# Batch 0's pooling in a written order, weights in halves and a new work list in an attention-and-maxout kernel

## The chip, the cores and the metric

The kernel runs on one core of one Trainium2 chip. The metric is the device time of one execution in microseconds (us); the median over several runs counts. Where a profile is read, times run from the start of its span. TensorE does the matrix products, VectorE and ScalarE the elementwise work, GpSimd and SyncE issue transfers (GpSimd adds some sums of its own).

## The reference, cut to what matters

```python
# x: (4, 12544, 128), inducing: (32, 128), w1, w2: (128, 1024), w_out: (1024, 128)
def mab(q, kv):
    s = scale * (q @ kv.transpose(0, 2, 1))       # scale = 1/sqrt(128)
    a = softmax(s)                                # over the rows of kv
    return a @ kv
h   = mab(inducing, x)     # pooling: 32 rows for each batch
y   = mab(x, h)            # each token attends to its batch's 32 rows
h1  = y @ w1
h2  = y @ w2
out = maximum(h1, h2) @ w_out                     # (50176, 128) float32
```

The kernel uses max(h1, h2) = h1 + relu(h2 - h1). The attention of a token over 32 rows is folded into the weights: for each batch, hwd = h (w2 - w1) is a 32 x 1024 matrix, and m1 = h w1 w_out a 32 x 128 one. What is left for a token are its 32 exponentials e, relu(e hwd) w_out + e m1, and a division by the sum of e at the end.

## The kernel before, in words

**Tiles.** A batch has 98 tiles of 128 tokens. Two buffers xT hold a batch's x turned (channels on the partitions), twelve tiles xn hold x as it comes, in 16 bits, each with 14 tiles of 128 tokens.

**Loading.** x comes by GpSimd's queue, which also makes 16 bits of it (`load_x`, L182). Batch 0 comes in eleven parts, `parts[0]` (L175): four of 14 tiles, four of 7, then 6, 5 and 3; the very first comes by SyncE and is cast by VectorE and ScalarE. Behind batch 0 the same queue loads w1, w2 and w_out (L240 to L242), then batch 1's seven parts (L765) and w1 and w2 once more in 32 bits (L548, L549), from which GpSimd makes w2 - w1 for the later batches.

**Batch 0's pooling** (L724 to L764) is the head of the kernel. For each part, `p1_transpose` turns it on TensorE (two halves, evicted by VectorE, L266, and ScalarE, L269), `p1_scores` multiplies with the 32 inducing rows and takes the exponential on ScalarE (L278, L287), and `p1_accum` sums up (L301 for the denominators, L310 for the rows of h). The parts go through these steps in a fixed pattern, with filling matmuls that compute nothing needed (`fill`, L720) between some of them. Then come the small steps: w1 is negated on VectorE (L768), `small_h` makes hT4 (h turned and repeated four times, L455), `weights_2` turns w1 in two groups of four blocks into w1T (L562), `small_sums` makes the reciprocals rs and rw (L481 to L486), `stage` makes the first e, and `small_hwd` the first half of hwd (L501 to L516).

**Batches 1 to 3** are pooled while the main work of the batch before runs. Their x is turned by transposing transfers of SyncE: `transpose_x_dma` (L200), eleven for each batch, x1.0 to x1.10 for batch 1, the first eight of 7 tiles, the last three of 14. `pool_scores` (c, L338) takes 16 tiles of xT at a time: c1.0 takes tiles 0 to 15, and x1.0, x1.1 and x1.2 bring tiles 0 to 6, 7 to 13 and 14 to 20. `pool_turn` (t) turns the exponentials with another transfer, `pool_accum` (a, L396) sums.

**Main work.** Up to 16 tiles form a block of four quarters. `stage` (s, L625) makes a block's e: TensorE multiplies in four column strips, ScalarE takes the exponential. `phase` (p, L1009) multiplies e with pieces of hwd in up to four row strips of TensorE at the same time; each unit fills a PSUM bank (128x512), and ScalarE (L1024) or VectorE (L1027) evicts it with a relu. p4 is a phase with four units, the figure behind the dot says which of its evictions change the engine. In phases with fewer than four units a strip may do the "linear" product e m1 for one group. `final_one` (L859) multiplies 128 columns of relu with a block of w_out: 3,136 of them, eight for each tile. When a group of up to four tiles is done, `evict_group` multiplies with the reciprocal of the sum on VectorE (L891) into one of five output tiles (`NOUT`), and SyncE stores it (L918). The sums of e come from another transposing transfer on SyncE (`turn_e2`, g, L651) and additions on GpSimd, or, for the first blocks, from TensorE (`dens`, L704).

**What sets the order.** All five engines run in a written order. The main work follows the word list `ORDER`: a number stands for so many final matmuls, a letter for a step (s, p, c, t, a, x, g as above; H the second half of batch 0's hwd; W, w, e, h, m small steps of weights and batches), and each word emits its instructions on every engine it uses, SyncE's queue too. A small model of the engines' times, `Clock`, is kept along the way: it chooses PSUM banks and eviction engines, and it says when filling matmuls are put in. Its estimates have no effect on the chip beyond that. The stores and all transposing transfers of SyncE stand in one queue, in the order of the list.

Of the kernel before, what the change touches and what calls it, by code (L numbers as in the profile page):

```python
# [16 lines left out]
INF = 1e9  # L17
NOUT = 5


class Clock:
# [4 lines left out]
    LAT = 0.20  # L26
    SEM = 0.05

    def __init__(self):
        self.pe = self.act = self.dve = self.sp = 0.0  # L30
        self.pool = self.loading = self.loaded = 0.0
        self.stored = [0.0] * NOUT
        self.mode = "full"
        self.bank = [0.0] * 8
        self.idle = {}
        self.log = []
        self.busy = {}
# [45 lines left out]
class Block:  # L83


    def __init__(self, quarters, full=()):
# [3 lines left out]
        self.staged = None  # L90
        self.divided = 0.0
# [32 lines left out]
def kernel(  # L124
# [50 lines left out]
    parts[0] = [(0, 14), (14, 14), (28, 14), (42, 14), (56, 7), (63, 7), (70, 7), (77, 7), (84, 6), (90, 5), (95, 3)]  # L175
# [41 lines left out]
    w1h = relup.tile([128, 4096], F16, name="w1h", tag="relu1")[:, 0:J]  # L217
    w21 = consts.tile([C, J], F16, name="w21")
    woutp = consts.tile([128, NJB, C], F16, name="woutp")
    w1T = consts.tile([128, NJB, C], F16, name="w1T")  # L220
# [6 lines left out]
    with tc.manual_schedule(engines={ET.PE, ET.DVE, ET.Activation, ET.Pool, ET.SP}):  # L227
# [12 lines left out]
        nc.gpsimd.dma_start(out=w1h, in_=moe_w1)  # L240
        nc.gpsimd.dma_start(out=w2h, in_=moe_w2)
# [11 lines left out]
        def p1_transpose(b, i, between=0):  # L253
            k0, n = parts[b][i]
            xn = xn_at[b, i]
            h = min(8, (n + 2) // 2)
            for g, m in ((0, h), (h, n - h)):
                if g and between:
                    fill(between)
                bi, ps = bank([128, 8, 128], F16)  # L260
                for j in range(m):
                    nc.tensor.transpose(ps[:, j, :], xn[:, g + j, :], identity16)  # L262
                end = ck.run(0.056 * m, ready=ck.bank[bi], why="T")
                dst = xT_tiles[b % 2][:, k0 + g : k0 + g + m, :]
                if g == 0:
                    nc.vector.tensor_copy(out=dst, in_=ps[:, 0:m, :])  # L266
                    ck.bank[bi] = ck.on_dve(end, 0.08 + 0.075 * m)
                else:
                    nc.scalar.copy(out=dst, in_=ps[:, 0:m, :])  # L269
                    ck.bank[bi] = ck.on_act(end, 0.05 + 0.12 * m)  # L270
                st[b]["xT", i] = max(ck.bank[bi], st[b].get(("xT", i), 0.0))

        def p1_scores(b, i):
# [11 lines left out]
            end = ck.run(0.029 * n)  # L285
# [5 lines left out]
        def p1_accum(b, i, lo=0, hi=P1):  # L291
# [4 lines left out]
            if b == 0:  # L296
# [20 lines left out]
                st[0]["end"] = ck.run(0.029 * (hi - lo) + 0.03 * ((hi - lo + 3) // 4))  # L317
# [132 lines left out]
        def small_h(b):  # L450
            hT4 = smp.tile([C, 4, M], F16, name=f"hT4_{b}", tag="hT4")
            if b == 0:
# [9 lines left out]
                st[b]["hT4r"] = ck.on_dve(st[0]["end"], 0.3)  # L462
# [3 lines left out]
                ready = ck.on_act(st[0]["end"], 0.2)  # L466
# [10 lines left out]
        def small_sums(es, ready):  # L477
# [9 lines left out]
            ck.bank[st[0]["eb"]] = st[0]["rsr"] = ck.on_dve(end, 0.34)  # L487

        def small_hwd(b, halves=(0, 1), vector=False):
            if 0 in halves:  # L490
                st[b]["hwd"] = smp.tile([128, J], F16, name=f"hwd_{b}", tag="hwd")
            hwd = st[b]["hwd"]
            for half in halves:
                for n in range(2 if b == 0 and half == 0 else 1):
                    w = 256 if b == 0 and half == 0 else 512
                    bi, ps = bank([128, 512])
                    ps = ps[:, 0:w]
                    sl = slice(512 * half + w * n, 512 * half + w * (n + 1))
                    ck.wait(max(ck.bank[bi], st[b]["hT4r"]), "p1")
                    if b == 0:  # L500
                        nc.tensor.matmul(out=ps, lhsT=st[b]["hT4"], rhs=w2h[:, sl], start=True, stop=False)  # L501
                        nc.tensor.matmul(out=ps, lhsT=st[b]["hT4"], rhs=w1h[:, sl], start=False, stop=True)
                        end = ck.run(0.43 * w / 512)
                    else:
                        nc.tensor.matmul(out=ps, lhsT=st[b]["hT4"], rhs=w21[:, sl], start=True, stop=True)  # L505
                        end = ck.run(0.215)
                    if half == 0 and n == 0 or vector:
                        if b == 0:
                            nc.vector.tensor_scalar(
                                out=hwd[:, sl], in0=ps, scalar1=st[0]["rw"], scalar2=None, op0=ALU.mult  # L510
                            )
                        else:
                            nc.vector.tensor_copy(out=hwd[:, sl], in_=ps)
                        ck.bank[bi] = ck.on_dve(end, 0.07 + w / 970.0)
                    else:
                        nc.scalar.activation(  # L516
                            out=hwd[:, sl], in_=ps, func=AF.Copy, scale=st[0]["rw"] if b == 0 else 1.0
                        )
                        ck.bank[bi] = ck.on_act(end, 0.06 + w / 1200.0)
                    st[b]["hw", half] = max(ck.bank[bi], st[b].get(("hw", half), 0.0))  # L520
# [35 lines left out]
        def weights_2():  # L556
            for g in range(2):
                bi, ps = bank([128, 4, 128], F16)
                ck.wait(ck.bank[bi], "w")
                for j in range(4):  # L560
                    jb = 4 * g + j
                    nc.tensor.transpose(ps[:, j, :], w1h[:, 128 * jb : 128 * (jb + 1)], identity16)  # L562
                end = ck.run(0.056 * 4)
                if g == 0:
                    nc.vector.tensor_copy(out=w1T[:, 0:4, :], in_=ps)
                    ck.bank[bi] = ck.on_dve(end, 0.4)
                else:
                    nc.scalar.copy(out=w1T[:, 4:8, :], in_=ps)
                    ck.bank[bi] = w_of["w1T"] = ck.on_act(end, 0.5)
# [41 lines left out]
        def stage(blk):  # L611
# [29 lines left out]
            blk.staged = ck.bank[bi] = ck.on_act(end, 0.05 + wd * 128 / 1200.0)  # L641

# [89 lines left out]
        for i in range(4):  # L732
            p1_transpose(0, i, 2 if i == 0 else 0)
            if i < 3:
                fill(2 - i // 2)
            if i == 0:
                bi, ps = bank([128, 512])
                nc.tensor.transpose(ps[:, 0:M], ind_sb, identity32[0:M, 0:M])
                nc.vector.tensor_copy(out=inducingT, in_=ps[:, 0:M])
                ck.bank[bi] = 0.0  # L740
                nc.vector.reduce_sum(out=diag, in_=identity32.rearrange("p (k m) -> p m k", m=M), axis=AX.X)
                for dst, f in ((rep32, DOWN / scale), (repd, 1.0)):
                    nc.vector.tensor_scalar(
                        out=dst.rearrange("p (k m) -> p k m", m=M),
                        in0=diag[:, None, :].broadcast_to((128, 4, M)),
                        scalar1=f,
                        scalar2=None,
                        op0=ALU.mult,
                    )
            if i > 0:  # L750
                p1_accum(0, i - 1)
            p1_scores(0, i)
        last = len(parts[0]) - 1
        p1_transpose(0, 4)
        p1_accum(0, 3)
        p1_transpose(0, 5)
        p1_scores(0, 4)
        for i in range(6, last + 1):
            p1_transpose(0, i)
            p1_scores(0, i - 1)  # L760
            p1_accum(0, i - 2)
        p1_scores(0, last)
        p1_accum(0, last - 1)
        p1_accum(0, last)  # L764
# [18 lines left out]
        for n, g in enumerate(groups):  # L783
            g.blk.last_group[g.q] = n
        state.update({"g": 0, "mm": 0, "done": 0, "issued": 0})
# [95 lines left out]
        def evict_group(g, end):  # L881
# [3 lines left out]
            qs = sorted({q for q, _ in g.chunks})  # L885
            per = n // len(qs)
            t0 = g.chunks[0][1]
            rp = g.blk.rp[:, t0 : t0 + per, qs[0] : qs[-1] + 1]
            if len(qs) == 1:
                rp = rp.broadcast_to((128, per, C))  # L890
                nc.vector.tensor_mul(osb[:, 0:n, :], g.ps[:, 0 : n * C].rearrange("p (s c) -> p s c", s=n), rp)  # L891
            elif per == 1:
                rp = g.blk.rp[:, t0, qs[0] : qs[-1] + 1]
                nc.vector.tensor_mul(
                    osb[:, 0:n, :],
# [227 lines left out]
```

## Time and profile before

| | |
|---|---|
| median of 3 runs | 317.46 us (317.13 to 318.28) |
| the profiled execution | 318.49 us, its span 316.7 us |
| TensorE busy | 311.5 us, 98% of the span |
| ScalarE busy | 279.0 us, 88% |
| VectorE busy | 273.6 us, 86% |
| GpSimd busy | 127.5 us, 40% |
| matmuls | 5,309, of them 3,136 finals |
| last sum of batch 0's pooling ends | 22.48 us |
| first final matmul | 26.89 us |
| granted TensorE clock | 1.00 |

In lists of instructions a line gives start, duration, engine, source line, operation, what it writes and reads, and a count. "PEld" is TensorE's load of weights, which lies beside its matmuls; "SPq" is SyncE's queue of transfers: the time there is that of issuing, not of the transfer. A line of busy times by stretch has, for TensorE, its weight loads, VectorE, ScalarE and GpSimd, the busy microseconds (with the number of instructions), then the granted clock, the DMA share and GB/s. A line of the chain gives start, duration and what the end of the program hung on at that time. Lines of DMA queues give packets, MB and share of 16 engines; q0 is GpSimd's queue and q1 is SyncE's.

### The profile page before, as it was taken

The numbers are of one execution on the slowest core, as the hardware profiler recorded it, in microseconds if no ns is written. First come the engines' busy times: TensorE is split into PE (matmuls) and PEld (weight loads), VectorE is DVE, ScalarE is ACT, GpSimd is POOL, SyncE is SP. The second block draws the span as 40 slices with busy tenths as digits, with TensorE's granted clock in tenths as the row PEclk, the third lists the DMA queues.
The fourth block names the chain that finished last, engine by engine and source line by source line (L and its number), as shares of the span: only waits on it lengthen the run. The fifth ranks groups of instructions, "written<-read, shape, count | busy, mean of one in ns | idle before, by whom it ended". The sixth has DMA issues, their size and how long they took to land.

```text
span 316.7 us, 12562 instructions
## 1 busy us (share of the span) xinstructions
PE 311.5 (98%) x5309; PEld 240.8 (76%) x5309; DVE 273.6 (86%) x486; ACT 279.0 (88%) x571; POOL 127.5 (40%) x189
## 2 busy tenths in 40 slices
PE   8999999999999999999999999999999999999996
PEld 3885767777877768778777787887868777787885
DVE  2348989999888899998988998889899989989995
ACT  2669999999999999998999989999899999998881
POOL 7442071648510066067320064449305663461500
PEclk9999999999999999999999999999999999999999
DMA  8999999999699998997399998995423233324223
GB/s 205 209 206 212 226 232 213 225 239 217 120 215 244 234 175 175 198 234 205 113 216 243 179 248 212 229 187 169 139 85 118 85 120 118 119 79 146 104 103 117
DMA packets 81480, 56.34 MB, mean 178 GB/s; under 512 B 62832, under 2 KB 66064, under 8 KB 81424
## 3 DMA queue, kind: packets, MB, share of 16 engines
q1 hardware_dynamic: 75312, 41.32, 56.6%
q0 software_dynamic: 6112, 14.22, 23.1%
q8 instruction: 41, 0.67, 1.0%
q14 instruction: 15, 0.12, 0.1%
HBM read 28.33 MB, written 25.69 MB: 171 GB/s over the span
## 4 chain that ended last, share of the span: by engine, by line
PE 95%; ACT 1%; DMA 1%; DVE 1%; issue 1%; DVEq 0%; ACTq 0%
PE ps L859 61%; PE ps L1009 23%; PE ps L625 2%; PE ps L262 2%; PE ps L338 2%; PE ps L396 1%; DMA xf<-in_x_dram 1%; PE ps L278 1%; PE ps L310 1%; PE ps L720 1%; PE ps L301 1%; PE ps L505 0%; PE ps L441 0%; ACT hwd L516 0%; ACT relu L1024 0%
## 5 line engine op out<-in xcount | busy, mean ns | idle before, releaser
L1024 ACT ACTIVATE relu<-ps 128x512 f16<-128x512 f32 x472 | 242.9, 619 | 20.8 <-PE ps L1009 18.9
L1027 DVE TENSOR_SCALAR relu<-ps 128x512 f16<-128x512 f32 x312 | 198.5, 684 | 19.4 <-PE ps L1009 18.6
L859 PE MATMUL ps<-woutp,relu 128*128 128x128 f16 x3136 | 204.0, 219 | 0.0
L859 PEld LDWEIGHTS <-relu 128*128 128x128 f16 x3136 | 176.6, 98 | 34.2 <-issue 28.7
L1009 PE MATMUL ps<-e,hwd 32*128 32x512 f16 (+2 forms) x880 | 85.3, 357 | 0.0
L660 POOL TENSOR_TENSOR half<-ed 128x256 f32<-128x256 f16 (+2 forms) x23 | 14.1, 613 | 126.9 <-DMA ed<-e 126.6
L664 POOL TENSOR_TENSOR rd<-den,minus 128x16 f32<-128x16 f32 (+2 forms) x23 | 60.7, 2639 | 1.9
L891 DVE TENSOR_TENSOR o<-ps,rd 128x512 f32<-128x512 f32 (+1 forms) x88 | 55.5, 633 | 4.1 <-PE ps L1009 2.4
L1009 PEld LDWEIGHTS <-hwd 32*128 32x128 f16 x880 | 28.0, 91 | 18.4 <-issue 5.1
L1009 PE MATMUL ps<-m,e 32*128 32x128 f16 x382 | 38.5, 216 | 0.0
L1009 PEld LDWEIGHTS <-e 32*128 32x128 f16 x382 | 22.6, 92 | 5.4 <-issue 1.7
L660 POOL TENSOR_TENSOR half<-half 128x32 f32<-128x32 f32 (+3 forms) x69 | 22.3, 323 | 5.4
L187 POOL DMA_DIRECT2D xn<-in_x_dram x31 | 17.0, 557 | 7.3 <-DMA xn<-in_x_dram 4.5
L891 DVE TENSOR_TENSOR o<-ps,rp 128x512 f32<-128x512 f32 (+3 forms) x20 | 12.9, 644 | 1.1 <-DMA out_dram<-o 0.8
L266 DVE COPY xT<-ps 128x512 f16<-128x512 f16 (+3 forms) x11 | 5.5, 504 | 8.3 <-PE ps L262 8.1
L637 ACT ACTIVATE e<-ps 128x512 f16<-128x512 f32 (+2 forms) x21 | 11.0, 596 | 0.2 <-PE ps L625 0.2
L351 ACT ACTIVATE eu<-ps 128x512 f16<-128x512 f32 x18 | 11.1, 615 | 0.1
L269 ACT COPY xT<-ps 128x768 f16<-128x768 f16 (+3 forms) x11 | 6.1, 557 | 3.6 <-PE ps L262 3.4
L625 PE MATMUL ps<-xT,hT 128*32 128x512 f16 (+3 forms) x114 | 8.8, 363 | 0.1
L262 PE MATMUL ps<-identity,xn 128*128 128x128 f16 x98 | 7.8, 226 | 0.1
L262 PEld LDWEIGHTS <-xn 128*128 128x128 f16 x98 | 6.0, 101 | 1.7 <-DVE xn L724 1.0
L338 PE MATMUL ps<-xT,inducingT 128*32 128x512 f16 x72 | 7.1, 386 | 0.0
(100 smaller groups left out, 112.4 us busy)
## 6 DMA issues: line engine op xcount, KB each, us to landing
out_dram<-o SPq DMA_DIRECT2D x90, 256.0 KB, 2.7
xn<-in_x_dram POOLq DMA_DIRECT2D x24, 448.0 KB, 11.8
out_dram<-o SPq DMA_DIRECT2D x10, 128.0 KB, 2.6
xn<-in_moe_w_dram POOLq DMA_DIRECT2D x4, 256.0 KB, 14.0
xn<-in_x_dram POOLq DMA_DIRECT2D x4, 224.0 KB, 9.6
xT<-xn SPq DMA_TRANSPOSE x33, 4.4
xf<-in_x_dram SPq DMA_DIRECT2D x1, 512.0 KB, 3.7
xf<-in_x_dram SPq DMA_DIRECT2D x1, 384.0 KB, 4.2
```

The source lines that it names most:

```text
L187: nc.gpsimd.dma_start(out=xn_at[b, i][:, 0:n, :], in_=xr[b, :, k0 : k0 + n, :])
L262: nc.tensor.transpose(ps[:, j, :], xn[:, g + j, :], identity16)
L338: nc.tensor.matmul(out=ps[32 * g : 32 * (g + 1), :], lhsT=inducingT, rhs=xT_tiles[b % 2][:, U * u + 4 * g : U * u + 4 * (g + 1), :], start ...
L351: nc.scalar.activation(out=eu, in_=ps, func=AF.Exp, scale=scale, accum_out=st[b]["es"][:, u : u + 1])
L625: nc.tensor.matmul(out=ps[32 * q : 32 * (q + 1), 128 * t : 128 * (t + n)], lhsT=hq, rhs=xT[:, c : c + n, :], start=True, stop=True, tile_p ...
L660: nc.gpsimd.tensor_tensor(out=dst, in0=cur[:, :, 0:n], in1=cur[:, :, n : 2 * n], op=ALU.add)
L664: nc.gpsimd.tensor_tensor(out=rp[:, 0:wd, :].rearrange("p t q -> p (t q)"), in0=den[:, 0 : 4 * wd], in1=minus1[:, 0 : 4 * wd], op=ALU.pow,)
L859: nc.tensor.matmul(out=g.ps[:, 128 * c : 128 * (c + 1)], lhsT=g.blk.relu[g.q][:, 128 * (jb * w4 + t) : 128 * (jb * w4 + t + 1)], rhs=woutp ...
L891: nc.vector.tensor_mul(osb[:, 0:n, :], g.ps[:, 0 : n * C].rearrange("p (s c) -> p s c", s=n), rp)
L1009: nc.tensor.matmul(**seq[i])
L1024: nc.scalar.activation(out=dst, in_=src, func=AF.Relu)
L1027: nc.vector.tensor_scalar(out=dst, in0=src, scalar1=0.0, scalar2=None, op0=ALU.max)
```

## The change

1. Batch 0 comes in twelve parts: the last three of 6, 5 and 3 tiles become four of 6, 4, 2 and 2. Its pooling follows a written list, `HEAD` (1a is the first half of part 1's transposes, S1 its scores, A1 its sum, I the inducing rows, N the negation of half of w1). Two of the seven filling matmuls stay.
2. w1 and w2 come in two halves each, and w1 is negated in halves (`negate`). w1T lies in the unused part of w1's buffer, and `weights_2` is split into a half before the list and a half in its first word, H.
3. Batch 0's hwd is made in three pieces of 256, 256 and 512 columns, the first two before the list, all evicted by VectorE. The first block's e is made in two halves of 256 columns (`stage_first`), and a unit waits for the half and the pieces that it reads.
4. `phase` writes the matmuls of its strips in the order in which their banks and inputs come free by the model, instead of in turn.
5. `evict_group` gives six of 107 groups to ScalarE (up to four activations of 128 columns each) by a written string, `EVICT`. There are six output tiles.
6. `ORDER` is a new list. The model's figures are changed too (landing times of batch 0's and batch 1's x, some durations).

The core of the diff:

```diff
-NOUT = 5
+NOUT = 6
...
-    parts[0] = [(0, 14), (14, 14), (28, 14), (42, 14), (56, 7), (63, 7), (70, 7), (77, 7), (84, 6), (90, 5), (95, 3)]
+    parts[0] = [(0, 14), (14, 14), (28, 14), (42, 14), (56, 7), (63, 7), (70, 7), (77, 7), (84, 6), (90, 4), (94, 2), (96, 2)]
...
-            st[b]["ld", i] = ck.loaded = max(ck.pe, 14.0) + 8.0 + 2.7 * i
+            st[b]["ld", i] = ck.loaded = ck.pe + 8.0 + 2.7 * i if b > 1 else 26.2 + 2.3 * i
...
-        nc.gpsimd.dma_start(out=w1h, in_=moe_w1)
-        nc.gpsimd.dma_start(out=w2h, in_=moe_w2)
+        for h in range(2):
+            sl = slice(512 * h, 512 * (h + 1))
+            nc.gpsimd.dma_start(out=w1h[:, sl], in_=moe_w1[:, sl])
+            nc.gpsimd.dma_start(out=w2h[:, sl], in_=moe_w2[:, sl])
...
+        p1_transpose(0, 0, 0)
+        fill(2)
+        p1_transpose(0, 0, 1)
+        HEAD = """
+        1a 1b I S0 2a 2b S1 A0 S2 3a 3b A1 4a 4b S3 S4 A2 A3 5a 5b A4 6a 6b S5 7a 7b S6 A5 8a 8b S7
+        A6 9a 9b 10a S8 11a N A7 S9 S10 A8 S11 A9 A10 A11
+        """
...
         for i in range(7):
             load_x(1, i)
         weights_1()
-        nc.vector.tensor_scalar(out=w1h, in0=w1h, scalar1=-1.0, scalar2=None, op0=ALU.mult)
         sums = small_h(0)
-        weights_2()
+        weights_2(0)
         small_sums(*sums)
-        stage(blocks[0])
         small_hwd(0, (0,))
+        stage_first(blocks[0])
+        negate(1)
+        small_hwd(0, (1,))
+        weights_2b(0)
...
+        def second_half(vector):
+            small_hwd(0, (2,), bool(vector))
+            weights_2(1)
+            weights_2b(1)
...
+            who = int(EVICT[g.index])
+            m = (n, 0)[who]
...
+            for k in range(m, n):
+                nc.scalar.activation(
+                    out=osb[:, k, :],
+                    in_=g.ps[:, k * C : (k + 1) * C],
+                    func=AF.Copy,
+                    scale=g.blk.rp[:, t0 + k, q : q + 1],
+                )
...
-            for i in range(4):
-                for seq in parts_:
-                    if i < len(seq):
-                        nc.tensor.matmul(**seq[i])
+            while any(seq for _, _, _, seq in parts_):
+                q, ready, us, seq = min(
+                    (p for p in parts_ if p[3]), key=lambda p: max(ck.issue, ck.tile[p[0]], p[1])
+                )
+                ck.issue = max(ck.issue, ck.tile[q], ready)
+                ck.tile[q] = ck.issue + us
+                nc.tensor.matmul(**seq.pop(0))
...
         ORDER = """
-        H0 o p4.5 s W p4.2 s 4 m0 4 p2.1 3 p3.2 1 g2 4 p2 8 p3.3 p2 14 p3.1 4 p4.1 6 x1.0 16 p2.1 p4.10
-        16 x1.1 x1.2 p4.4 4 g1 12 p4.9 12 p4.11 p1 19 p3.4 p2 14 p4 s s 3 x1.3 x1.4 4 x1.5 x1.6 7 p3.5 s
-        s g3 8 p4.10 27 p3 p4.2 18 p3.2 14 p3 6 p4.4 12 x1.7 3 x1.8 x1.9 c1.0 p1 p4.4 13 g4 1 p4.5 15
+        H1 o p4.11 s s W 3 p4.8 p2 g2 1 m0 10 p3 p2.1 10 p3.2 p2 11 p3 7 p4 21 p2 p4.10 17 x1.0 p4.9 4 g1
+        12 p4.1 12 p4.8 p1 4 x1.1 4 x1.2 x1.3 11 p3 p2.1 14 p4.10 13 p3.6 s s s s 6 g3 6 p4.6 14 p4 14
+        p4.4 15 c1.0 p2.2 p3.2 x1.4 3 x1.5 x1.6 x1.7 x1.8 4 x1.9 13 p4.9 11 x1.10 5 p1.1 p4 11 p4.4 g4 16
...
```

Batch 2's first two transposes, x2.0 and x2.1, stand behind 816 and 820 finals in the list before, behind 752 and 754 in the new one; c2.0 stands behind 920 and 921.

More of the change, by code (lines that the diff above doesn't have):

```diff
@@ L26 @@
     LAT = 0.20
+    ROW = 0.224
     SEM = 0.05
@@ L32, in __init__ @@
         self.stored = [0.0] * NOUT
+        self.issue, self.tile = 0.0, [0.0] * 4
         self.mode = "full"
@@ L256, in p1_transpose @@
             h = min(8, (n + 2) // 2)
[L257 to L271, printed above, removed]
+            g, m = ((0, h), (h, n - h))[half]
+            assert m
+            bi, ps = bank([128, 8, 128], F16)
+            for j in range(m):
+                nc.tensor.transpose(ps[:, j, :], xn[:, g + j, :], identity16)
+            end = ck.run(0.0555 * m, ready=max(ck.bank[bi], LANDED[i] + 0.1), why="T")
+            dst = xT_tiles[b % 2][:, k0 + g : k0 + g + m, :]
+            if half == 0:
+                nc.vector.tensor_copy(out=dst, in_=ps[:, 0:m, :])
+                ck.bank[bi] = ck.on_dve(end, 0.08 + 0.067 * m)
+            else:
+                nc.scalar.copy(out=dst, in_=ps[:, 0:m, :])
+                ck.bank[bi] = ck.on_act(end, 0.05 + 0.108 * m)
+            st[b]["xT", i] = max(ck.bank[bi], st[b].get(("xT", i), 0.0))
         def p1_scores(b, i):
@@ L491, in small_hwd @@
                 st[b]["hwd"] = smp.tile([128, J], F16, name=f"hwd_{b}", tag="hwd")
             hwd = st[b]["hwd"]
[L493 to L499, printed above, removed]
+            for step in steps:
+                lo, hi = cuts[step]
+                w, sl = hi - lo, slice(lo, hi)
+                bi, ps = bank([128, 512])
+                ps = ps[:, 0:w]
+                ck.wait(max(ck.bank[bi], st[b]["hT4r"], w_of["neg", lo // 512] if b == 0 else 0.0), "p1")
+                if b == 0:
+                    nc.tensor.matmul(out=ps, lhsT=st[b]["hT4"], rhs=w2h[:, sl], start=True, stop=False)
+                    nc.tensor.matmul(out=ps, lhsT=st[b]["hT4"], rhs=w1h[:, sl], start=False, stop=True)
+                    end = ck.run(0.43 * w / 512)
+                else:
+                    nc.tensor.matmul(out=ps, lhsT=st[b]["hT4"], rhs=w21[:, sl], start=True, stop=True)
+                    end = ck.run(0.215)
+                if vector if b == 0 else step == 0:
@@ new lines @@
+        ck.pe = ck.act = ck.dve = 5.3
+        p1_transpose(0, 0, 0)
+        fill(2)
+        ck.pe, ck.act = 7.18, 6.25
+        p1_transpose(0, 0, 1)
[3 more added lines that the diff above has]
+        """
+        for word in HEAD.split():
+            if word == "I":
+                head_ind()
+            elif word == "N":
+                negate(0)
+            elif word[0] == "S":
+                p1_scores(0, int(word[1:]))
+            elif word[0] == "A":
+                p1_accum(0, int(word[1:]))
+            else:
+                p1_transpose(0, int(word[:-1]), "ab".index(word[-1]))
```

274 lines of the change are left out of this document (139 added, 135 removed).

## The prediction

> **What bounds the kernel.** I read the page's busy table and chain first, then busy time by stretch, then the chain of waits piece by piece, and last SyncE's timeline with the landing times of single transposes.
>
> Busy table and chain of the page:
> ```profile
> PE 311.5 (98%) x5309; PEld 240.8 (76%) x5309; DVE 273.6 (86%) x486; ACT 279.0 (88%) x571; POOL 127.5 (40%) x189
> PE 95%; ACT 1%; DMA 1%; DVE 1%; issue 1%; DVEq 0%; ACTq 0%
> ```
> Busy time by stretch (from 27 to 40 and from 40 to 52 us):
> ```profile
> 27.00:40.00 13.00, 12.97 (x203) 9.18 (x201) 12.54 (x25) 12.79 (x27) 1.08 (x2) 1.00 1.08 225
> 40.00:52.00 12.00, 12.00 (x187) 8.40 (x185) 11.00 (x19) 11.91 (x25) 7.34 (x8) 1.00 1.21 223
> ```
> TensorE sets the end. Its chain after 27 us has no hole worth a microsecond: a run of 27 final matmuls takes 1.61 us and one of 38 takes 2.23, so one costs 0.0565 us and each change into the run 0.09; a phase alone costs 0.33 and a second one behind it about 0.22. Only two things can shorten it: an earlier start, and fewer changes between kinds of matmul. ScalarE (98%) and VectorE (92 to 96%) follow close behind.
>
> The start, in the chain from 22 to 27.5 us:
> ```profile
> 22.39 0.09 PE ps L310 x3
> 22.47 0.46 PE ps L562 x8
> 23.10 0.51 PE ps L625 x4
> 24.21 1.07 ACT hwd L516 x2
> 25.28 0.98 ACT relu L1024 x2
> 26.89 0.38 PE ps L859 x4
> ```
> Batch 0's pooling ends at 22.48, the first final matmul starts at 26.89; between them the chain goes through ScalarE.
>
> SyncE's timeline, and the landing of three transposes, of x1.0 (issued 34.6), x1.1 (40.1) and x1.2 (43.0), each asked for alone:
> ```profile
> 29.28 1.29 SPq L651 DMA_TRANSPOSE ed<-e  x1
> 30.63 3.94 SPq L918 DMA_DIRECT2D out_dram<-o  x2
> 34.61 4.79 SPq L200 DMA_TRANSPOSE xT<-xn  x1
> 40.07 5.67 SPq L200 DMA_TRANSPOSE xT<-xn  x2
> ```
> ```profile
> DMA to landing us min/median/max: 12.2/12.2/12.2
> DMA to landing us min/median/max: 8.0/8.0/8.0
> DMA to landing us min/median/max: 6.0/6.0/6.0
> ```
> They landed at 46.8, 48.1 and 49.0. DMA queues between 32 and 42 us:
> ```profile
> q0 software_dynamic: 669, 2.13, 85.9%
> q1 hardware_dynamic: 963, 0.47, 21.3%
> ```
> GpSimd's loads (q0) hold the DMA engines until 42.3 (the last one issued at 30.43, 11.9 us to landing); SyncE's queue (q1), which also carries the stores, gets 963 packets in those ten microseconds, mostly of 256 bytes, three for every two large ones of the loads. In the 6.5 us after 42.5 it gets 2,724. Where pooling of batch 1 needs them:
> ```profile
> 51.43 0.40 PE L338 MATMUL ps<-xT,inducingT 128*32 128x512 f16 x4
> ```
> c1.0, the first scores of batch 1, reads tiles 0 to 15, and tiles 14 and 15 come with x1.2. Before, x1.2 is there 2.4 us early.
>
> **The pooling order (HEAD).** Fourteen tiles cost TensorE 0.79 (transposes) + 0.35 (scores) + 0.62 (sums) = 1.76 us. Today's last part (issued 9.95, 9.6 us to landing) is there at 19.55, but its transposes start at 20.70: five of seven filling matmuls (0.22 each) and two waits for ScalarE (0.81 and 0.55 in the chain) put TensorE behind. The new order drops those five fills and moves each sum behind later transposes, so it should be at the last part soon after it lands, 19.7. From there the old chain took 1.78 us for three tiles; two take a little less, 1.5. Pooling ends at 21.2 instead of 22.5: 1.3 us earlier. Bounds: 0.7 if a ScalarE wait comes back, 1.8 if data lands earlier.
>
> **Weights in halves, hwd in three pieces, first tile in halves.** The same bytes, three more GpSimd issues (two weight halves, one part of x) at 0.53 = 1.6 us. Queued behind them on GpSimd are batch 1's loads, the first issued at 15.67 and landing at 25.7, 2.2 us apart; issued some 3 us later it still has a queue in front of it (the weights end at 23.4). Nothing on the path; if that cover is gone, up to 1 us of loads. Today w1h lands at 20.8 and w2h at 21.9; the first halves would be there by about 20.9, ahead of the first hwd matmul (about 21.7). VectorE takes all three hwd evictions (0.48 + 0.48 + 0.7) plus the negation (0.42 today for all) and one w1T copy (0.42): 2.5 us in a row from 22.2, against 0.48 on VectorE and 1.07 on ScalarE now. ScalarE is freed for the exponentials, so the first phase can go at about 23.9 (24.49 now). The three finals before the list's first sum then come near 25.6, one phase fewer done: worth 1.2 us against now. Bounds 0.6 and 1.8.
>
> **The list as work.** Counted word by word, finals stay 3,136, phases go from 249 to 250, changes between kinds of matmul from 377 to 370: +0.22 - 0.7 = -0.5 us. But it is dealt out anew around c1.0: 209 finals, 22 phases and 10 fewer changes ahead of it, where 243 and 25 stood. That is 34 x 0.0565 + 3 x 0.22 + 10 x 0.1 = 3.6 us less, minus 0.23 for four w1 transposes that move into the list: 3.35. TensorE reaches c1.0 at 51.43 - 1.2 - 3.35 = 46.9 us. Behind c1.0 stand 34 finals, 4 phases and a change more: +2.9 us.
>
> **The new wait.** c1.0 cannot start before x1.2 has landed, and that hangs on the loads. Batch 1 cannot arrive much sooner, since the same bytes stand ahead of it. On SyncE, x1.0 has 80 finals before it instead of 48, in time about 34 us as now; with 116 finals, not 80, before x1.2, one store more (256 KB, about 0.65 us at the 400 GB/s of that stretch) lies ahead of it; g2's transpose goes about 2.4 us earlier (behind 3 finals and two phases less, 1.2 us, in a list that starts 1.2 us earlier), which brings some 130 of the slow early packets forward (0.3 us); the split weights may cost 0.2. So x1.2 lands at 49.0 + 0.65 - 0.3 + 0.2 = 49.5, say 49.3 since a store can fall into the pauses after 42.5. TensorE waits 2.4 us. Queued behind c1.0 on TensorE is everything, phases and finals; ScalarE and VectorE run dry after a microsecond. Bounds: 46.9 (no wait), if the backlog drains at the 982 packets per us seen at best, from 50 to 51, and 50.5, if the ring is as slow as for x1.0.
>
> **Other parts.** The phases' matmuls in the order in which banks come free: same instructions, TensorE still ends with the last one; 0, between -0.5 and +0.5, nearest the row of ScalarE's idle time behind phases, which lies off the path. Six evictions on ScalarE as four 128-column copies (0.30 for the nearest row, w1out): 1.2 instead of 0.65 on VectorE, hidden by whichever of the two has room; 6 x 0.55 = 3.3 if neither has. A sixth output tile ends a known wait:
> ```profile
> DVE o L891 <- DMA out_dram<-o: 0.9, 2, 0.8
> ```
> It lies on VectorE; I take 0.2 on the path.
>
> **Sum.** From c1.0 to the end of the span now: 316.7 - 51.43 = 265.3. After: 49.3 + 265.3 + 2.9 - 0.2 = 317.3, 0.6 more than 316.7. The profiled execution took 318.49, 1.79 us more than its span, and lies 1.03 above the median of 317.46. So 319.1 for a profiled run, and 318.1 as median. The head's 1.2 us are inside the wait.
>
> **Rivals.**
> Faster: x1.2 lands by 47.1, so c1.0 waits 0.2 at most. Then the gains count: 1.2 + 0.5 + 0.2 = 1.9, 315.6 with no wait and 315.8 with 0.2. For it: g2 goes earlier, and most of a microsecond three times over between 43 and 47 the queue stood still. Against it: x1.2 landed 6.0 us after its issue with the loads already gone, and q0 ends no earlier.
>
> Slower: in batch 2, x2.0 and x2.1 go behind 752 finals instead of 816, about 101 us instead of 108.5, while that batch's loads run until 108. x1.0 under loads took 12.2 us; these would land near 112, and every store behind them in SyncE's queue waits. Stores there already need 7.8 us (median, 90 to 108) and a group is due every 2.7 us: 3 outstanding + 4 new against six tiles. From the seventh on VectorE stands, and relu with it: 2.5 us on top of the forecast, 320.6. Against it: 6 tiles just about hold.
>
> Clock: TensorE's granted clock is 1.00 in all stretches, and its longest wait after the start is 0.3 us, so nothing here shows what a long one does. At the start the matmuls run slow for 6.0 us: from 1.19 on a filling one takes 0.63, later 0.38, and up to 7.2 eight transposes take 1.03 where six take 0.50 afterwards. If a wait of 3.6 us (landing at 50.5) brought such a stretch back at half speed, that is 1.2 + 3.0 us on top: 322.3. [...]
>
> The head not getting earlier at all changes nothing, as long as c1.0 is reached before 49.3.
>
> **Chances.** Forecast case 0.50 (316.0 to 319.0), faster rival 0.22, slower rival 0.23, clock 0.05. The range reaches from 315.0 (no wait and the upper bound of the start, 0.6 more) to 320.8, just past the slower rival. About 0.5%, 1.6 us, is what a measurement of this kernel can tell from no change. Faster by more 0.22, within 0.50, slower by more 0.28.
>
> **What would show it.** Pooling's last sum near 21.2; the first finals near 25.6; a wait of TensorE for a DMA on xT at the scores line, of some 2.4 us, right where batch 1's scores begin near 49.3; x1.2 landing then; no other wait above a microsecond; phases 250. The forecast is wrong if that wait is missing, if a wait for out_dram above 2 us appears near 110, or if phases and finals cost other than 0.33 and 0.0565.

## The result

The kernel after the change takes 318.79 us (median of 6 runs, 318.18 to 319.84), the kernel before 317.48 (6 runs): a ratio of 1.0040, 95% interval 1.0020 to 1.0059. It is 1.3 us slower: inside the half per cent that I had called no change, but with an interval that lies clear of 1. The forecast was 318.1, in a range from 315.0 to 320.8. The profiled execution of after took 319.84 us with a span of 318.1, 1.4 more than the span of before; it is the slowest of the six and the only one in which the clock fell (mean granted clock 0.995, in the others 0.999 or more), and their median span is 317.0.

### The profile page after: what moved, and what is told of

Read it like the earlier page. It is cut to its first block, busy times and chain, and to the rows that moved or that the text cites. A ratio compares the mean times of both kernels' runs of the same rounds, so it can differ in the third digit from the quotient of the medians.

```text
span 318.1 us, 12582 instructions
## 1 busy us (share of the span) xinstructions
PE 311.5 (98%) x5308; PEld 241.0 (76%) x5308; DVE 273.9 (86%) x486; ACT 281.4 (88%) x582; POOL 129.0 (41%) x192
## 4 chain that ended last, share of the span: by engine, by line
PE 89%; DMA 5%; POOL 1%; SPq 1%; DVE 1%; ACT 1%; issue 1%; POOLq 0%; DVEq 0%
PE ps L914 58%; PE ps L1067 22%; DMA xn<-in_x_dram 4%; PE ps L646 2%; PE ps L345 2%; DMA xT<-xn 2%; PE ps L403 1%; POOL xn L190 1%; SPq L203 1%; DVE relu L1087 1%; ACT relu L1084 1%; PE ps L269 1%; PE ps L516 0%; PE ps L317 0%; PE ps L448 0%
## 5 line engine op out<-in xcount | busy, mean ns | idle before, releaser
L1067 PE MATMUL ps<-e,hwd 32*128 32x512 f16 (+2 forms) x840 | 82.8, 361 | 0.0
L946 DVE TENSOR_TENSOR o<-ps,rd 128x512 f32<-128x512 f32 (+3 forms) x82 | 52.6, 643 | 5.5 <-PE ps L1067 2.2
L1067 PE MATMUL ps<-m,e 32*128 32x128 f16 x372 | 37.0, 216 | 0.0
L1067 PEld LDWEIGHTS <-hwd 32*128 32x128 f16 x880 | 26.9, 91 | 12.8 <-issue 3.6
L646 PE MATMUL ps<-xT,hT 128*32 128x512 f16 (+3 forms) x110 | 8.1, 373 | 0.0
L345 PE MATMUL ps<-xT,inducingT 128*32 128x512 f16 x72 | 7.7, 386 | 0.4 <-DMA xT<-xn 0.4
```

Source lines behind the costliest of these rows:

```text
L345: nc.tensor.matmul(out=ps[32 * g : 32 * (g + 1), :], lhsT=inducingT, rhs=xT_tiles[b % 2][:, U * u + 4 * g : U * u + 4 * (g + 1), :], start ...
L646: nc.tensor.matmul(out=ps[32 * q : 32 * (q + 1), 128 * t : 128 * (t + n)], lhsT=hq, rhs=xT[:, c : c + n, :], start=True, stop=True, tile_p ...
L946: nc.vector.tensor_mul(osb[:, 0:m, :], g.ps[:, 0 : m * C].rearrange("p (s c) -> p s c", s=m), g.blk.rp[:, t0 : t0 + m, q : q + 1].broadcas ...
L1067: nc.tensor.matmul(**seq.pop(0))
```

## The profile after

The busy table and the chain of the page, and busy time by stretch (27 to 40 and 40 to 52 us):
```profile
PE 311.5 (98%) x5308; PEld 241.0 (76%) x5308; DVE 273.9 (86%) x486; ACT 281.4 (88%) x582; POOL 129.0 (41%) x192
PE 89%; DMA 5%; POOL 1%; SPq 1%; DVE 1%; ACT 1%; issue 1%; POOLq 0%; DVEq 0%
```
```profile
27.00:40.00 13.00, 12.99 (x205) 9.16 (x202) 12.27 (x24) 12.88 (x28) 1.09 (x3) 1.00 1.08 211
40.00:52.00 12.00, 11.64 (x177) 8.21 (x175) 10.44 (x18) 10.98 (x24) 7.33 (x8) 1.00 1.11 262
```
TensorE's busy time is the same, 311.5 us. What is new is the 5% of DMA in the chain, and a hole on TensorE between 40 and 52 us, in which VectorE and ScalarE lose half a microsecond to one microsecond too. Of the DMA, 11.5 us are one load of batch 0's x, which the pooling now follows closely, and 5.1 us are x1.2, which is at issue here.

The start, in the chain from 21 to 27.6 us:
```profile
21.46 0.15 PE ps L317 x2
...
22.66 0.48 ACT e_first L684
...
23.19 0.40 PE ps L673 x3
23.59 0.33 PE ps L512
23.92 0.21 PE ps L513
24.13 0.43 PE ps L512
...
27.42 0.19 PE ps L914 x3
```
And from TensorE's timeline, the second half of the first score tile:
```profile
23.19 0.40 PE L673 MATMUL ps<-xT,hT 128*32 128x256 f16 x4 [0.58 <-ACT e_first L684]
```
Pooling ends at 21.61, but the first final starts at 27.28 (the chain has its end alone, from 27.42), 0.4 later than before. Two things lie between. The two halves of the first score tile sit in the same PSUM bank, so the second half's matmuls (L673) wait 0.58 us for ScalarE to empty the first (L684). And a 512-column matmul of hwd (L512, L513) takes 0.43 us where its like took 0.22: the granted clock had fallen to one half. Two stretches by busy time show it, in the last figure but two:
```profile
19.72:23.13 3.41, 2.89 (x54) 2.31 (x51) 2.02 (x9) 1.65 (x7) 3.41 (x8) 1.00 1.32 162
23.13:26.55 3.42, 3.36 (x29) 1.53 (x28) 2.21 (x5) 1.58 (x4) 1.17 (x4) 0.51 1.08 213
```

SyncE's timeline, the landing of x1.0 (issued 37.66), x1.1 (41.9) and x1.2 (45.1), each asked for alone, and the DMA queues between 32 and 42 us:
```profile
30.67 6.87 SPq L971 DMA_DIRECT2D out_dram<-o  x4
37.66 3.56 SPq L203 DMA_TRANSPOSE xT<-xn  x1
41.38 0.46 SPq L971 DMA_DIRECT2D out_dram<-o  x1
41.89 6.69 SPq L203 DMA_TRANSPOSE xT<-xn  x3
```
```profile
DMA to landing us min/median/max: 9.8/9.8/9.8
DMA to landing us min/median/max: 7.5/7.5/7.5
DMA to landing us min/median/max: 5.1/5.1/5.1
```
```profile
q0 software_dynamic: 680, 2.20, 92.6%
q1 hardware_dynamic: 686, 0.20, 14.7%
```
The three landed at 47.5, 49.4 and 50.2 us, against 46.8, 48.1 and 49.0 before. x1.0 went out three microseconds later and arrived only 0.7 later. In those ten microseconds SyncE's queue and GpSimd's got nearly the same number of packets, 686 and 680, but a packet of the loads has 3.2 KB on average and one of SyncE's 0.3 KB. In `e1_two_banks` the two counts are nearly the same too (679 and 672), but before had 963 and 669 in the same ten microseconds: how the DMA engines share themselves out between the two queues no run here settles.

The scores of batch 1 on TensorE's timeline, and what the chain has ahead of the second of these lines:
```profile
49.22 0.63 PE L345 MATMUL ps<-xT,inducingT 128*32 128x512 f16 x3
50.21 0.38 PE L345 MATMUL ps<-xT,inducingT 128*32 128x512 f16 x1 [0.36 <-DMA xT<-xn]
```
```profile
45.06 5.10 DMA xT<-xn
```
c1.0 is reached at 49.22, two microseconds earlier in time than before (51.43) although the finals began 0.4 later, and its strips wait for x1.1 and x1.2: the four matmuls take 1.4 us where 0.40 did before. From the last strip to the end of the span it is 318.1 - 50.21 = 267.9 us.

## The experiments

Two theories stood at first. S (in series): the end is the landing of x1.2 plus fixed work, so whatever the start loses or wins is swallowed by the wait at c1.0. T (start; the texts below call it rival H): the time lost at the start, 1.7 us against the forecast first final, is the time lost. Later two others took their place: L, the new list is what costs, and D, the new head's loads are.

**The start.** `e1_two_banks` gives each half of the first score tile its own bank:
```
-  ck.wait(max(ck.bank[bi], st[0]["hT4r"]), "stage bank")
+  ck.wait(max(ck.bank[bi], st[0]["hT4r"]), "stage bank"); ck.bank[bi] = INF
```


> The two halves of the first e get a PSUM bank each; the order of all instructions stays. Theory S (series: a late start, and behind it the wait of c1.0 for x1.2, which takes up most of what an earlier start brings): the 0.6 us wait for ScalarE goes, the clock stays at 1.00, the first final comes at 25.2 to 25.6 instead of 27.28, TensorE then reaches c1.0 about 47.3 and waits there some 2 us, since x1.2 lands at 49.3 to 49.8. The total falls by 0.4 to 0.9 us, to about 318.1. Rival H (the start alone makes the change slow): it falls by the whole 1.7 to 2.0 us, to about 316.9, and c1.0 waits no longer than now.

Measured: 318.70 us, ratio 1.0035 (1.0023 to 1.0047). The clock stays at 1.00 and the first final comes at 25.17, 2.1 us earlier than in the profile of after. More than half of it is gone 22 us later, when c1.0's last strip runs 0.9 earlier. TensorE's timeline at c1.0:
```profile
47.32 0.39 PE L345 MATMUL ps<-xT,inducingT 128*32 128x512 f16 x1
48.52 0.39 PE L345 MATMUL ps<-xT,inducingT 128*32 128x512 f16 x2 [0.81 <-DMA xT<-xn]
49.28 0.38 PE L345 MATMUL ps<-xT,inducingT 128*32 128x512 f16 x1 [0.36 <-DMA xT<-xn]
```
The first strip runs at 47.32, the last at 49.28: 1.9 us of waiting for two transfers. First final and wait are as S had them; the total of 318.1 that it expected did not come. Five of after's six executions had the clock up without this edit.

`e4_fill` leaves the shared bank and puts three filling matmuls of 512 columns into the gap:
```
-  ends.append((bi, ps, ck.run(0.113, "col")))
+  ends.append((bi, ps, ck.run(0.113, "col"))); h or fill_other(bi)
```


> The bank stays shared, but three filling matmuls of 512 columns (0.65 us) stand between the halves, so that TensorE is busy while it waits for ScalarE. Theory S with the clock as the larger part of the late start: granted clock 1.00 through 23 to 27 us, first final near 26.0 instead of 27.28; the total falls by 0.2 to 0.5 us, the rest goes into the wait at c1.0. Rival: the bank wait of 0.6 us is itself what delays the start and the clock follows from something else; first final stays at 27.0 or later and the granted clock still falls to 0.5.

Measured: 318.73 us, 1.0039 (1.0026 to 1.0052), clock 1.00, first final 26.17. So of the 2.1 us between the first finals of after (27.28) and e1 (25.17), 1.1 go with the halved clock and 1.0 with the shared bank and the fills. e1 and e4 begin their finals 1.0 us apart, x1.2 lands at 49.2 and 49.1, and they take 318.70 and 318.73: S holds for this microsecond, T falls. For the one execution with a first final at 27.28 it is not shown: there x1.2 landed at 50.2 and the total was 319.84, a microsecond more than in the others of after; why x1.2 came later is not traced.

**The wait.** `e2_late_c10` moves c1.0 36 finals down the list, past x1.4 to x1.10; `e3_both` does that with two banks:
```
-  p4.4 15 c1.0 p2.2 p3.2 x1.4 3 x1.5 ... x1.10 5 p1.1 p4 11
+  p4.4 15 p2.2 p3.2 x1.4 3 x1.5 ... x1.10 5 p1.1 p4 c1.0 11
```


> The word c1.0 moves back by some 30 finals, to where x1.2 has surely landed; nothing else. Theory S: the wait at the scores line (about 0.8 us together with the strips before it) goes, and the total falls by 0.5 to 0.8 us, to about 318.1. Rival H: TensorE loses nothing at c1.0 that it would not lose later; the total stays within 0.2 us of 318.8.

> Both edits. Theory S: now nothing holds the earlier start back; 1.8 + 0.7 = 2.5 us less than the changed kernel, about 316.3, that is 1.2 us faster than the kernel before. Both together bring clearly more than the sum of what each brings alone (0.7 + 0.7). Rival H: no more than the first edit alone, 316.9.

Measured: 319.42 (1.0058, 1.0044 to 1.0072) and 318.94 (1.0044, 1.0032 to 1.0057). The median of e2 says little beside that of after, since the clock fell in four of its six executions (mean granted 0.994 or 0.995) and in one of after's (0.995). Of the two profiled executions, both with the fallen clock (0.994 and 0.995), e2 needs 0.7 us less from the first final to the end (290.1 for 290.8 us), with no wait of TensorE for a transfer between 40 and 80 us: as much as S had expected, but one pair of executions. e3, with the clock up (1.00) and an earlier start, gained nothing, and S as I had put it, c1.0 alone, fell there. In e3 c1.0 runs at 51.23 with no wait, but 12.78 us pass between its 240th and its 360th final, where the same list takes 11.34 in e2: 1.4 us more. The chain of e3 in that stretch:
```profile
50.48 0.70 DVE o L946
...
51.31 1.26 SPq L203
...
52.63 1.32 SPq L203
...
54.04 5.07 DMA xT<-xn
...
59.14 0.39 PE ps L345 x2
```
x1.4, x1.5 and x1.6 are issued from 51.31 on, behind a store that waits for an eviction, and x1.6 lands at 59.1, where the last strips of c1.2 (L345) already wait for it. The list explains it: x1.4 stands behind 209 finals, x1.5 and x1.6 behind 212, where the list of before has them behind 144 and 148.

**List or loads.** Four more kernels, all with two banks. `e5_old_list` puts the list of before in place of the new one. `e6_whole_weights` loads w1 and w2 whole:
```
-  for h in range(2):
-      sl = slice(512 * h, 512 * (h + 1))
+  for h in range(1):
+      sl = slice(0, J)
```
`e7_early_x` moves x1.0 to x1.2 up, and `e8_late_w` moves the second load of w1 and w2 down:
```
-  7 p4 21 p2 p4.10 17 x1.0 p4.9 4 g1 12 p4.1 12 p4.8 p1 4 x1.1 4 x1.2 x1.3
+  7 p4 6 x1.0 15 p2 p4.10 17 x1.1 x1.2 p4.9 4 g1 12 p4.1 12 p4.8 p1 8 x1.3
```
```
-  weights_1()                       # ahead of the list
+  "o": lambda: (weights_1(), weights_1b()),   # and o behind g5 in the list
```


> The changed kernel with two banks for the first score tile, and with the list of before in place of the new one (the new head stays). Theory L, the new list issues batch 1's transposing transfers too late (x1.0 at 37.7 for 34.6 us, x1.4 at 52.2 for 49.9): with the old list x1.2 lands near 49.0 and x1.4 near 53.9 again, the finals start at 25.2 as in the kernel with two banks, and of the 1.7 us by which that is ahead of before some 1.0 to 1.5 is kept: 316.0 to 316.5. Theory D, the new head's loads (weights split, woutp and batch 1's loads landing 0.3 to 1.5 us later) hold the transfers: x1.2 lands at 49.3 or later in spite of the old list, and the time is that of before or more, 317.5 to 318.7.

> The changed kernel with two banks, and with w1 and w2 loaded by one DMA each again (negated and used in halves as in the change). Theory D: woutp and the loads of batch 1 end 0.6 us earlier, x1.2 lands near 48.7 and the kernel ends 0.5 us earlier than with two banks alone, 318.2. Theory L: the transfers are set by when SyncE issues them; no change, 318.7. Against both: the first final may come up to 0.5 us later, because the first half's negation now waits for the whole of w1.

> The changed kernel with two banks, and with x1.0 moved ahead by 15 finals and a mode change in the list, x1.1 and x1.2 to where x1.0 stood (as many finals from the start as in the list of before, within 20). Theory L: x1.0 is issued 1 to 2 us earlier, x1.2 lands 0.5 to 1 us earlier and the wait at c1.0 shrinks by as much; x1.3 and later stay, so the end moves by 0.5 us at most, 318.2 to 318.7. Theory D: the transfers issued earlier only wait longer beside the loads; x1.2 lands within 0.3 us of 49.3, no change, 318.7.

> The changed kernel with two banks, and with the second load of w1 and w2 (1.05 MB in four DMAs, 24 to 45 us) and their subtraction moved behind g5 of the list, some 30 us later: nothing is left out. Theory D: the last load ahead of batch 1's transfers lands at 41 instead of 45 us, x1.0 to x1.2 land 2 to 3 us earlier (x1.2 near 46.8), no wait at c1.0, and the end comes 1 to 2 us earlier: 317.0 to 317.7, or 318.2 if the load shows up as a wait where it now stands. Theory L: x1.2 lands earlier, but x1.4 and on, issued after 51 us, land where they did; the wait moves to c1.1 and c1.2, and the end moves by 0.3 us at most: 318.4 to 318.7.

Measured:

| kernel | x1.2 lands | wait at c1.0 | median, us | ratio (95%) |
|---|---|---|---|---|
| e1, two banks | 49.2 | 1.9 | 318.70 | 1.0035 (1.0023 to 1.0047) |
| e6, whole weights | 48.3 | 0.3 | 318.40 | 1.0020 (1.0010 to 1.0031) |
| e7, x1.0 to x1.2 earlier | 48.4 | 1.1 | 318.71 | 1.0031 (1.0019 to 1.0044) |
| e8, second weights later | 47.5 | 0.2 | 321.98 | 1.0148 (1.0129 to 1.0167) |
| e5, old list | 49.3 | none | 321.94 | 1.0140 (1.0124 to 1.0156) |

(The wait is the time of c1.0's four matmuls beyond 0.4 us.) With each of the three edits x1.2 does come earlier, by 0.9 to 1.8 us, as D expected of whole weights, L of an earlier place and both of a lighter load stream. In e6 c1.0 ends 0.9 us earlier than in e1 and so does the profiled kernel (span 316.2 for 317.1); the ratios to before show half a microsecond of it, with intervals that overlap, and in 5 of its 12 executions the clock fell (the last section; the other seven have a median of 318.00). In e7 0.7 us went straight to the next transfer of the pooling ("PE ps L403 <- DMA eT<-eu: 0.7, 1, 0.7" in its waits), and nothing is left in the median.

What sets the end shows best in five profiles that have c1.0 where the new list puts it and no wait behind it. x1.2 lands at 50.16, 49.24, 49.12, 48.31 and 48.21 us in after, e1, e4, e6 and `e11_whole_early` (below), and the spans are 318.08, 317.13, 317.01, 316.23 and 316.12: the landing plus 267.9 us each time. That is S.

e8 is the plainest case of a load that only moves: the megabyte taken from ahead of x1.0 now stands ahead of batch 2's loads, which go out 5.5 us later, and the waits on TensorE are these:
```profile
PE ps L345 <- DMA xT<-xn: 2.8, 1, 2.8
PE ps L403 <- DMA eT<-eu: 1.5, 1, 1.5
```
L had not asked where the load would stand next, and D had allowed for a wait there, but at 318.2: it cost more there than here.

e5 answers nothing by its median, since it has an accident of its own far behind. The chain at 228 us:
```profile
227.60 0.29 DVE hacc L436
227.89 3.07 DVE relu L1087 x5
```
A figure behind a phase's dot turns round the model's choice of eviction engine; with the changed model the old list's figures turn the wrong ones, and five relus stand ahead of a small step that everything waits for. Up to there e5 had kept level with the first profile of before: both had their 2,100th final at 224.4 us. So:

`e9_old_list_whole` is e5 with each relu on the engine that it has in before, and all 108 groups evicted by VectorE:
```
-  if (max(ck.act, ready) + 0.477 <= max(ck.dve, ready) + 0.597) != bool(flip >> k & 1):
+  if RELU[blk.index, q, t0, u]:        # the 784 choices of before
```
`e10_old_list_w` is e9 with whole weights, `e11_whole_early` e6 and e7 together, `e12_before_again` the kernel before.

> The changed kernel with two banks and the list of before, as in the run with the old list, and now also with that list's own choice of engine for each of the 784 relu evictions and with every group evicted by VectorE, as in before (in the run with the old list the changed clock model turned the list's flips round, and five relus stood in VectorE's queue at 228 us). What is left of the change is the head, the order in which row-tile matmuls are emitted, and NOUT 6. Theory L (the new list costs, the head brings a little): the stall at 228 us is gone, 3.1 us less than with the old list alone, and the end comes 0.2 to 0.5 us ahead of before: 317.0 to 317.5. Theory D (the new head's later loads cost what its earlier start brings): 317.7 to 318.3, no better than the new list with whole weights (318.4) by more than 0.5.

> The kernel of the run before it (old list with its own evictions, new head, two banks), with w1 and w2 loaded by one DMA each. Theory D: woutp and batch 1's loads end some 0.6 us earlier, x1.2 lands near 48.6 and 0.3 us are won, as with the new list: 0.3 less than the run before it. Theory L: the old list issues the transfers early enough either way; within 0.2 of the run before it. This is the version that could beat both kernels, at 316.8 to 317.4.

> The new list and two banks with both small edits that made x1.2 land earlier: w1 and w2 loaded whole, and x1.0 to x1.2 earlier in the list. Theory D: both shifts add up, x1.2 lands near 47.8, the wait at c1.0 falls to 0.5 us, and the end comes 0.5 us ahead of whole weights alone: 317.9. Theory L: x1.4 and later transfers and the transposes of the pooling's weights (eT<-eu), which stand where they did, take it back: 318.3 to 318.7.

> The kernel before, unchanged, for a second profile. Its profiled execution was 1.0 us longer than the median of its timed ones; the one step of that profile that stands alone is at 105 to 110 us, where VectorE waited 0.9 us for a store (out_dram). If that wait belongs to that execution alone, the second profile has no step there and a span near 315.8; if it is the kernel's, the step is there again and the span is 316.5 to 316.9.

Measured: e9 takes 317.32 us, 0.9989 (0.9974 to 1.0003). With the head, the halves and the emission order of the change kept, the two banks of e1, and only list and evictions taken back, the loss is gone. The chain of e9 has c1.0, c1.1 and c1.2 without a transfer ahead of them:
```profile
51.04 0.33 PE ps L345 x4
...
54.09 0.33 PE ps L345 x4
...
59.80 0.33 PE ps L345 x4
```
x1.2 lands at 49.0 in e9, hardly earlier than the 49.2 of e1. The old list just keeps TensorE busy until 51.0 before it asks, and it has x1.3 to x1.6 issued in one row from 47.07 on. e1 and e9 differ in list and eviction engines alone, and their ratios to before by 0.46%, 1.5 us: that is the price of the new list with its evictions. In the profiles it is 1.9 us, and the wait at c1.0 in e1 has that size. What the head brings by itself, 0.11%, can't be told from nothing.

e10: 318.37 (1.0021, 1.0005 to 1.0037), 1.05 us more than e9, where 0.3 less had been expected. w2, issued at 14.51, now takes 8.0 us to land, at 22.5, and the first hwd matmul waits for it (the profile names VectorE's rw, which ended later; in e9 the same matmul went ahead of that). For the next 3.4 us TensorE runs at half clock. Its timeline and the two stretches:
```profile
22.68 0.37 PE L512 MATMUL ps<-w2h,hT 128*128 128x256 f16 x1 [0.49 <-DVE rw L493]
```
```profile
19.00:22.40 3.40, 3.19 (x73) 2.85 (x69) 1.86 (x7) 2.00 (x8) 2.37 (x5) 1.00 1.41 198
22.40:25.80 3.40, 3.12 (x26) 1.46 (x27) 1.66 (x5) 1.40 (x3) 1.07 (x2) 0.52 1.10 214
```
Here nothing swallows it, because the old list has no wait at c1.0: its first final is at 28.02 against e9's 26.41. The clock is the smaller part of the loss: the three executions in which it did not fall have a median of 318.28, still 1.0 us above e9, and the first hwd matmul alone starts 0.8 later than there (22.68 for 21.88).

e11: 318.08 (1.0005, 0.9988 to 1.0023). x1.2 lands at 48.2, not 47.8, and c1.0 still ends 0.4 late; of D's 317.9 most came. It is the best version found with the new list, and no better than before. It keeps the new list's evictions, so most of that list's price lay in the transfers and not in the evictions.

e12: its profile has no wait for out_dram near 110, and a span of 316.0, so that wait belonged to the first execution alone. Final by final, the first execution falls 0.3 us behind this one between 105 and 109 us; the other 0.4 of the 0.7 by which their spans differ are lost elsewhere.

## Why the prediction was right, and where not

The total came out 0.7 us above the forecast, and the mechanism was the one named: a list that reaches c1.0 early meets a transfer that is not there. Part of the agreement is luck. In the profiled execution the finals began 1.7 us late, so the wait at c1.0 was 1.0 us and not 2.4, and c1.0 was reached at 49.22, hardly ahead of the 49.3 that the prediction had made a condition.

- **Pooling order:** ends at 21.61; forecast 21.2, bounds 20.7 to 21.8. A gain of 0.9 for 1.3.
- **First finals near 25.6: wrong.** 27.28. The step that failed is the sum from pooling's end to the first phase, which took the first tile's halves as free of each other. They share a bank, and the wait that this makes (0.58 us) was followed by a half-speed stretch (granted clock 0.51 for 3.42 us). With both removed (e1) they come at 25.17, a little better than the forecast. With the clock up and fills in the gap (e4) they come at 26.17.
- **The list as work:** from the first final to c1.0 it is 47.32 - 25.17 = 22.15 us in e1, and was 51.43 - 26.89 = 24.54 before, 2.4 less. The forecast was 46.9 - 25.6 = 21.3, 3.2 less. The step that failed is the price of a phase. Taken from the starts of the matmuls in that stretch, the finals fall from 15.75 to 13.35 us, but the phases, though fewer, go from 7.60 to 7.75: in e1 the first two pairs of them behind the first final, on the first tile in halves, take 1.22 and 0.82 us, where the prediction's prices (0.33 and 0.22) give 0.55 for a pair. Whether that is their short matmuls or a wait that the modelled ends hide is not traced.
- **x1.2 at 49.3:** 50.2 in the profiled execution of after, 0.9 more, which is the whole miss of its span (318.1 for 317.3). In the profiles with the clock up it landed as forecast, at 49.2 (e1, with a wait of 1.9 us for 2.4) and 49.1 (e4), with spans of 317.1 and 317.0. The terms behind it did not hold one by one: x1.0 was to be issued at about 34 as before and went out at 35.8 in e1, and the split weights were given 0.2, where loading them whole moved x1.2 by 0.9 (e6), though other things move with it.
- **From the span to the median:** this is the term that was mis-sized in the total. The median span of after, 317.0, is 0.3 below the forecast span. The forecast then took off the 1.03 us by which before's profiled execution lay above its median, as if all of it sat in what was carried over; measured, the median lies as far above the median span as the profiled execution above its own, 1.8 us. The second profile of before, near its median, has a span 0.7 shorter than the first.
- **Behind c1.0:** 267.9 us for 265.3 + 2.9 - 0.2 = 268.0. Right in sum, in part by luck: in e12 the same stretch of before takes 264.8 and has no wait for out_dram, so the list costs 3.1 there and the sixth output tile had nothing to win.
- **"The head not getting earlier at all changes nothing"**: right for the microsecond between e1 and e4.
- **Faster rival:** fell; x1.2 never came before 47.4, even with a megabyte less ahead of it (e8). **Slower rival:** fell; no wait for out_dram from 100 to 116 us. In e8, where batch 2's loads were pushed back, TensorE did wait 2.8 us for that batch's x, which is another wait than the one feared. **Clock rival:** half speed did come, but at the start and without a long wait (0.58 us at most in the 3.41 us ahead of it); the wait at c1.0, 1.9 us in all in e1 (0.81 at a stretch), cost no clock, and neither did the 2.8 us in e8's profiled execution (mean granted clock 1.00 in both). That the forecast put no loss of clock on its wait of 2.4 us, and the chance of 0.05, were estimates of mine; what a wait of 3.6 us does no run shows.

What the prediction did not see is the second half of the list's cost. It read x1.0 to x1.2 and c1.0, and not that x1.4 to x1.6 stand 65 finals later than before; with c1.0 out of the way (e3) that holds 1.4 us.

## What to carry to other kernels

When a work list is dealt out anew, compare for each transfer the work ahead of its issue and the work ahead of its use, one by one through the batch: removing one wait only shows the next. A gain ahead of a point that a transfer sets is worth nothing until that transfer comes earlier, and the small transfers of this kernel, beside its large loads, hardly do: x1.0 issued 3 us later landed 0.7 later (after against before), and issued 2.1 us earlier it brought x1.2 forward by 0.9 (e7 against e1). And choices tuned to one cost model, like the flips here, need not carry over to another: in e5 they put 3.1 us into one place.

## What was not expected of the hardware

TensorE's clock fell to one half for 3.41 us, with no long wait ahead of it. In after it had been full for 17.07 us, five times that length, and in the last 3.41 us before the fall TensorE was busy for 2.92 us (86%), its longest wait 0.58 us; in e10 it was 3.08 of 3.41 (90%), with the wait of 0.49 just at the end. In e1 and in e4, with its filling matmuls, the clock stayed up (1.00 in both profiles). The first two lines are from after, the third is from e6, where the clock did not fall; the stretches are counted off in 3.41 us, as long as the one at half clock, from the change to full clock at the start of each profile (6.03 us in after, 3.90 in e6):
```profile
6.03:9.44 3.41, 2.58 (x39) 1.89 (x38) 1.82 (x5) 1.82 (x3) 1.42 (x3) 1.00 1.08 214
19.69:23.10 3.41, 2.92 (x56) 2.34 (x52) 2.02 (x9) 1.65 (x7) 3.41 (x8) 1.00 1.32 162
20.97:24.38 3.41, 2.93 (x37) 1.83 (x35) 2.02 (x8) 1.22 (x4) 1.25 (x3) 1.00 1.34 207
```
So the busy share of such a stretch does not decide: after the first line (76%) and after the third (86%, longest wait 0.48 us) the clock stayed at 1.00. Whether the size of the matmuls counts (1 and 32 columns in much of the second line) no run here settles.

The same kernel does not always do it: the mean granted clock was 0.993 to 0.995 in 1 of 6 runs of after, 4 of 6 of e2, 5 of 12 of e6, 9 of 12 of e10 and 4 of 12 of e11 (in 1 of 8 of e12 too), and 0.998 or more in their others; in e8 it was 0.989 to 0.995 in 4 of 5, where in the run is not traced. In e6 those five have a median of 318.69, the other seven one of 318.00, and in e11 it is 318.67 against 318.00: 0.7 us.

In after the clock stood at half for 3.41 us, at full for 17.07 ahead of that; in before it stood at full for 310.61, from 6.96 us on to past the end of its span: about 1, 5 and 91 times 3.41. What sets these lengths, and why the runs of one kernel differ, no run here shows.
